# Gated linear attention and a squareplus MLP: logarithms a group ahead, second-layer PSUM banks of their own, smaller groups

## The chip, the cores and the metric

One core of a Trainium2 chip. The metric is the device time of one execution in microseconds. The engines are TensorE (PE, with its weight loads PEld), VectorE (DVE), ScalarE (ACT), GpSimd (POOL) and SyncE (SP), which here only issues DMAs.

## The reference

Attention with a decaying state, 4 batches of 8 heads, 768 steps, 48 dimensions, then an MLP with the activation squareplus:

```python
f = 1.0 / (1.0 + np.exp(-f_logit))
for t in range(S):
    state = f[:, :, t, :, None] * state + np.einsum('bhd,bhe->bhde', k[:, :, t], v[:, :, t])
    y[:, :, t] = np.einsum('bhd,bhde->bhe', q[:, :, t], state)
x = y.transpose(0, 2, 1, 3).reshape(3072, 384)
h = x @ w_in                                   # 384 x 2048
out = (0.5 * (h + np.sqrt(h * h + 4.0))) @ w_out   # 2048 x 384
```

## The kernel before

The 3072 tokens are 24 row blocks of 128 steps (6 for a batch), handled as 12 pairs. A recurrence over a block is a chunked matmul form: with the logarithms of the decays summed over the block, q is multiplied by one exponential and k by its inverse, and scores, state update and outputs are matmuls.

The stages of a pair:

- *Loads* (`load_pair`, L96): f, q, k and v, eight DMAs of 192 KB on SP, into four buffers each.
- *Logarithms* (`exp_ln`, L131): two ACT passes, Exp in place and Ln into `ls`, then on DVE the fp16 cast `hi` (L137, tile lhi) and the rest `lo` (L138, tile llo); POOL casts v to `v16` (L140).
- *Decays* (`cums`, L143): PE sums hi and lo within a block (L148, L149) into two of the four PSUM banks `hps`; ACT takes `ea` (L155) and `eap` (L156) from them, POOL multiplies q and k with these (L157, L158); PE then forms boundary sums in the same banks (L164, L165), DVE copies them to `nls` (L166).
- *Gammas* (`gammas`, L168), once for a group: a small DVE addition `gi` (L180) and two small Exp on ACT, `gam` (L183), which scale the state from block to block.
- *Attention* of a block, in steps that stand in slots (`attention`, L264): transposes T with an eviction to qkT (L205 to L208), scores SC with a mask multiplication pm on DVE (L218, L220), state KV (L229 to L235), outputs Y (L246 to L251), transposed back by YT (L258, L261). Every one of T, SC (twice), KV, Y, YT takes one of the four PSUM banks of the pool `pp_a`.
- *First layer* (`mlp1`, L288): for a pair 8 halves of 6 matmuls (L299) into the four hps banks; after each two halves ACT squares (L306) and takes the root (L307), and DVE forms the activation g (L310).
- *Second layer* (`mlp2`, L317): 32 matmuls (L328) in 8 quarters into an accumulator `o`, also from `pp_a`, a copy to `o_sb` (L332) and a store on SP (L334).

The pairs are in groups (`GROUPS`). For each group there is a *window* (`run_window`, L366): ACT loads the table with Exp and Ln (L367), does logarithms, decays and gammas of the group, and loads the table with Sqrt (L371). Between windows stands the *stretch* of first layers (`run_mlp1`, L376) of the group before; attention slots of the group just prepared are dealt out between its halves. Second-layer quarters wait in the list `fill`: two are issued at each step of a window, and before a pair's first layer as many as bring the list down to 24.

The order on ACT is that of the code (`manual_schedule`). The other engines and SP have a compile-time planner, which plays the program through with estimated durations and issues what is ready, older code first. Every queue is then fixed and runs in that order. Groups count row blocks: `(4, 6)` is pair 2. Windows are called here by the group's number, so that window 3 is that of pairs 3 and 4 before.

Of the kernel before, what the change touches and what calls it, by code (L numbers as in the profile page):

```python
# [14 lines left out]

GROUPS = [(0, 2), (2, 4), (4, 6), (6, 10), (10, 16), (16, 22), (22, 24)]
# [3 lines left out]
def kernel(  # L22
# [34 lines left out]
    pp_a = ctx.enter_context(tc.tile_pool(name="pp_a", bufs=4, space=PSUM))  # L57
# [20 lines left out]
    qt = [konst.tile([128, PR, H, 64], FP16, name=f"qt{i}") for i in range(NB)]  # L78
    kt = [konst.tile([128, PR, H, 64], FP16, name=f"kt{i}") for i in range(NB)]
    lhi = [konst.tile([128, PR, H, 64], FP16, name=f"lhi{i}") for i in range(2)]  # L80
    llo = [konst.tile([128, PR, H, 64], FP16, name=f"llo{i}") for i in range(2)]
# [43 lines left out]
    def window(g):  # L125

        r0, r1 = GROUPS[g]
        pairs = range(r0 // PR, r1 // PR)
        lss, steps = {}, []

        def exp_ln(p):  # L131
            f = loads[p]["f"]
            ls = wp.tile([128, PR, H, D], FP32, name="ls", tag="ls")
            nc.scalar.activation(out=f, in_=f, func=AF.Exp, scale=-1.0)
            nc.scalar.activation(out=ls, in_=f, func=AF.Ln, bias=1.0, scale=1.0)
            hi, lo = lhi[p % 2], llo[p % 2]
            nc.vector.tensor_copy(out=hi[:, :, :, 0:D], in_=ls)  # L137
            nc.vector.tensor_tensor(out=lo[:, :, :, 0:D], in0=ls, in1=hi[:, :, :, 0:D], op=ALU.subtract)  # L138
            v16 = bp.tile([128, PR, H, D], FP16, name="v16", tag="v16", bufs=4)
            nc.gpsimd.tensor_copy(out=v16, in_=loads[p]["v"])  # L140
            v16s[p] = v16

        def cums(p):  # L143
            hi, lo = lhi[p % 2], llo[p % 2]
            hp2 = [hps[2 * (p % 2) + r] for r in range(PR)]
            for r in range(PR):
                ca = hp2[r][:, 0:H * D]
                nc.tensor.matmul(out=ca, lhsT=wcent, rhs=hi[:, r, :, 0:D], start=True, stop=False)  # L148
                nc.tensor.matmul(out=ca, lhsT=wcent, rhs=lo[:, r, :, 0:D], start=False, stop=True)  # L149
            ea = wp.tile([128, PR, H, D], FP32, name="ea", tag="ea")  # L150
            eap = wp.tile([128, PR, H, D], FP32, name="eap", tag="eap")
            ld = loads[p]
            for r in range(PR):
                ca = hp2[r][:, 0:H * D]
                nc.scalar.activation(out=ea[:, r].rearrange("p h d -> p (h d)"), in_=ca, func=AF.Exp, scale=-1.0)  # L155
                nc.scalar.activation(out=eap[:, r].rearrange("p h d -> p (h d)"), in_=ca, func=AF.Exp, scale=1.0)  # L156
            nc.gpsimd.tensor_tensor(out=qt[p % NB][:, :, :, 0:D], in0=ld["q"], in1=ea, op=ALU.mult)  # L157
            nc.gpsimd.tensor_tensor(out=kt[p % NB][:, :, :, 0:D], in0=ld["k"], in1=eap, op=ALU.mult)  # L158
            b, c = divmod(p * PR, NC)
            for r in range(PR):  # L160
                nl = hp2[r][:, H * D:H * D + 2 * NP].rearrange("p (j s) -> p j s", s=2)
                for hp in range(NP):
                    o = nl[:, hp, :]
                    nc.tensor.matmul(out=o, lhsT=hi[:, r, 2 * hp:2 * hp + 2, :], rhs=hvec, start=True, stop=False)  # L164
                    nc.tensor.matmul(out=o, lhsT=lo[:, r, 2 * hp:2 * hp + 2, :], rhs=hvec, start=False, stop=True)  # L165
                nc.vector.tensor_copy(out=nls[b % 2][:, c + r], in_=nl)  # L166

        def gammas():  # L168

            a = r0  # L170
            while a < r1:
                b, c = divmod(a, NC)
                e = min(r1, (b + 1) * NC)
                n = e - a
                nb, gm = nls[b % 2], gam[b % 2]
                c0 = max(c - 1, 0)
                c1 = c + n - 1
                if c1 > c0:
                    gi = wp.tile([128, NC, NP], FP32, name="gi", tag="gi")
                    nc.vector.tensor_tensor(out=gi[:, c0:c1], in0=nb[:, c0:c1, :, 1],  # L180
                                            in1=nb[:, c0 + 1:c1 + 1, :, 0], op=ALU.add)
                    for s in range(2):
                        nc.scalar.activation(out=gm[64 * s:64 * s + 64, c0:c1, :, s],  # L183
                                             in_=gi[64 * s:64 * s + 64, c0:c1], func=AF.Exp, scale=-1.0)
                a = e

        ps = list(pairs)
        steps.append(lambda p=ps[0]: exp_ln(p))
        for i, p in enumerate(ps):
            if i + 1 < len(ps):  # L190
                steps.append(lambda p=ps[i + 1]: exp_ln(p))
            steps.append(lambda p=p: cums(p))
        steps.append(gammas)
        return steps

# [5 lines left out]
    def st_T(r):  # L201
        p, i = divmod(r, PR)
        tr = pp_a.tile([128, 2 * NP, C], FP16, name="tr", tag="a")
        for j in range(NP):
            nc.tensor.transpose(out=tr[:, j, :], in_=qt[p % NB][:, i, 2 * j:2 * j + 2, :], identity=ident16)  # L205
            nc.tensor.transpose(out=tr[:, NP + j, :], in_=kt[p % NB][:, i, 2 * j:2 * j + 2, :], identity=ident16)  # L206
        qkT = bp.tile([128, 2 * NP, C], FP16, name="qkT", tag="qkT")
        nc.vector.tensor_copy(out=qkT, in_=tr)  # L208
        part[r] = {"qkT": qkT}
# [243 lines left out]
```

## Time and profile before

| | us |
|---|---|
| median of 3 runs | 272.44 (270.02 to 272.85) |
| profiled execution, device time | 270.39 |
| its span, first to last instruction | 268.6 |
| PE busy | 213.1 |
| DVE busy | 182.7 |
| ACT busy | 169.3 |
| POOL busy | 57.5 |

Busy PE is not PE at its peak, since ends of matmuls are modelled and overlap. Times in rows count from the span's start. "Idle" beside an instruction is the time in which its engine waited just ahead of it, with what ended the wait.

### The profile page before, as it was taken

How to read it: one execution, taken by the hardware profiler on the slowest of the kernel's cores; microseconds unless marked ns; L12 is line 12 of the kernel's file. 1: busy time of each engine (PE TensorE's matmuls, PEld its weight loads, DVE VectorE, ACT ScalarE, POOL GpSimd, SP SyncE). 2: the span in 40 equal slices, each digit the busy share in tenths (PEclk: the TensorE clock that was granted, in tenths of full speed). 3: DMA queues.
4: the chain of work that ended last, by engine and by line, in shares of the span. 5: the costliest groups of instructions: out<-in, count | busy, mean ns of one | idle time of the engine just before them, and what ended most of it. 6: DMA issues, size and time to landing. Idle time of an engine off the chain costs nothing.

```text
span 268.6 us, 5160 instructions
## 1 busy us (share of the span) xinstructions
PE 213.1 (79%) x2024; PEld 148.9 (55%) x2024; DVE 182.7 (68%) x332; ACT 169.3 (63%) x252; POOL 57.5 (21%) x52
## 2 busy tenths in 40 slices
PE   0366939897688775986886869999886999999995
PEld 0143626664446553575664537777654777767652
DVE  1456726863583899579999666999983697645521
ACT  4355567884822956548968645988867795938200
POOL 4325001004209001494110396000005000000000
PEclk9999995999555997999999989999998899999999
DMA  8995599599995099999994000000000000010121
GB/s 144 187 220 184 161 234 302 153 245 188 177 216 93 8 214 185 187 217 195 166 199 76 31 32 29 2 0 4 2 29 29 2 29 33 29 59 32 59 79 70
DMA packets 107032, 30.22 MB, mean 113 GB/s; under 512 B 100352, under 2 KB 105472, under 8 KB 107008
## 3 DMA queue, kind: packets, MB, share of 16 engines
q1 hardware_dynamic: 107008, 29.89, 58.8%
q8 instruction: 16, 0.26, 0.4%
q14 instruction: 8, 0.07, 0.1%
HBM read 25.17 MB, written 4.72 MB: 111 GB/s over the span
## 4 chain that ended last, share of the span: by engine, by line
PE 32%; DVE 22%; ACT 16%; DMA 10%; issue 8%; SPq 6%; POOL 4%; POOLq 1%; ACTq 0%; DVEq 0%
PE o L328 16%; PE hps L299 10%; SPq L104 6%; DVE g L310 6%; ACT hsq L306 4%; DVE pm L220 3%; ACT r L307 3%; DMA ld_v<-in_v_dram 3%; DMA ld_f<-in_f_logit_dram 3%; DMA w_st<-in_moe_w_in_dram 3%; DVE qkT L208 2%; DVE llo L138 2%; POOL kt L158 2%; DVE y L251 2%; ACT L371 2%
## 5 line engine op out<-in xcount | busy, mean ns | idle before, releaser
L299 PE MATMUL hps<-xT,w_in 128*128 128x256 f16 x576 | 80.5, 285 | 10.6 <-DVE g L310 9.7
L310 DVE SCALAR_TENSOR_TENSOR g<-hps,r 128x512 f16<-128x512 f32 x96 | 61.8, 682 | 20.5 <-ACT r L307 20.5
L328 PE MATMUL o<-w_out,g 128*128 128x384 f16 x384 | 73.0, 335 | 0.2 <-DVE w_out L120 0.2
L299 PEld LDWEIGHTS <-w_in 128*128 128x128 f16 x576 | 57.0, 102 | 23.5 <-issue 13.2
L306 ACT ACTIVATE hsq<-hps 128x512 f16<-128x512 f32 x96 | 54.5, 590 | 23.4 <-PE hps L299 22.3
L307 ACT ACTIVATE r<-hsq 128x1024 f16<-128x1024 f16 x48 | 50.7, 1057 | 1.5
L328 PEld LDWEIGHTS <-g 128*128 128x128 f16 x384 | 37.6, 100 | 23.4 <-issue 3.3
L157 POOL TENSOR_TENSOR qt<-ld_q,ea 128x768 f16<-128x768 f32 x12 | 22.7, 1892 | 82.4 <-ACT ea L155 72.6
L220 DVE TENSOR_TENSOR pm<-sc,mask 128x512 f16<-128x512 f32 x48 | 30.9, 682 | 4.2 <-PE sc L218 4.2
L155 ACT ACTIVATE ea<-hps 128x384 f32<-128x384 f32 x24 | 11.9, 494 | 29.1 <-PE hps L149 29.1
L140 POOL CAST v<-ld_v 128x768 f16<-128x768 f32 x12 | 10.2, 853 | 65.6 <-DMA ld_v<-in_v_dram 60.7
L332 DVE COPY o_sb<-o 128x384 f32<-128x384 f32 x24 | 13.2, 554 | 16.0 <-PE o L328 16.0
L158 POOL TENSOR_TENSOR kt<-ld_k,eap 128x768 f16<-128x768 f32 x12 | 22.4, 1866 | 0.0
L208 DVE COPY qkT<-tr 128x1024 f16<-128x1024 f16 x24 | 16.4, 682 | 8.8 <-PE tr L206 8.8
L205 PE MATMUL tr<-ident,qt 128*128 128x128 f16 x96 | 16.7, 245 | 4.6 <-POOL qt L157 3.8
L206 PE MATMUL tr<-ident,kt 128*128 128x128 f16 x96 | 16.3, 246 | 4.7 <-POOL kt L158 4.7
L218 PE MATMUL sc<-qkT 48*128 48x128 f16 x192 | 12.1, 243 | 7.2 <-DVE qkT L208 7.1
L166 DVE COPY nls<-hps 128x8 f32<-128x8 f32 x24 | 3.8, 163 | 19.6 <-PE hps L165 18.6
L148 PE MATMUL hps<-lhi,wcent 128*128 128x384 f16 x24 | 8.2, 394 | 10.4 <-DVE wcent L66 8.7
L248 PE MATMUL y<-v,pm 128*128 128x48 f16 x192 | 14.1, 193 | 2.7 <-DVE pm L220 2.5
L183 ACT ACTIVATE gam<-gi 64x8 f32<-64x8 f32 (+2 forms) x18 | 3.8, 209 | 17.5 <-DVE gi L180 17.4
L206 PEld LDWEIGHTS <-kt 128*128 128x128 f16 x96 | 10.6, 111 | 7.5 <-POOL kt L158 5.8
(49 smaller groups left out, 256.0 us busy)
## 6 DMA issues: line engine op xcount, KB each, us to landing
ld_f<-in_f_logit_dram SPq DMA_DIRECT2D x24, 192.0 KB, 4.6
ld_q<-in_q_dram SPq DMA_DIRECT2D x24, 192.0 KB, 4.6
ld_k<-in_k_dram SPq DMA_DIRECT2D x24, 192.0 KB, 4.6
ld_v<-in_v_dram SPq DMA_DIRECT2D x24, 192.0 KB, 4.6
out_dram<-o_sb SPq DMA_DIRECT2D x24, 192.0 KB, 1.9
w_st<-in_moe_w_in_dram SPq DMA_DIRECT2D x4, 768.0 KB, 6.2
w_st<-in_moe_w_out_dram SPq DMA_DIRECT2D x4, 768.0 KB, 5.3
```

The costliest lines, as they stand in the source:

```text
L104: nc.sync.dma_start(out=got[name][:, r], in_=src[b][:, c * C:(c + 1) * C, :].rearrange("h t d -> t h d"))
L157: nc.gpsimd.tensor_tensor(out=qt[p % NB][:, :, :, 0:D], in0=ld["q"], in1=ea, op=ALU.mult)
L158: nc.gpsimd.tensor_tensor(out=kt[p % NB][:, :, :, 0:D], in0=ld["k"], in1=eap, op=ALU.mult)
L205: nc.tensor.transpose(out=tr[:, j, :], in_=qt[p % NB][:, i, 2 * j:2 * j + 2, :], identity=ident16)
L206: nc.tensor.transpose(out=tr[:, NP + j, :], in_=kt[p % NB][:, i, 2 * j:2 * j + 2, :], identity=ident16)
L208: nc.vector.tensor_copy(out=qkT, in_=tr)
L220: nc.vector.tensor_tensor(out=pm[:, s], in0=sc, in1=mask16.unsqueeze(1).broadcast_to([128, NP, C]), op=ALU.mult)
L299: nc.tensor.matmul(out=hb[:, a, :], lhsT=w_in16[:, j, jn * 128:(jn + 1) * 128], rhs=x[:, j, :], start=(j == 0), stop=(j == NJ - 1))
L306: nc.scalar.activation(out=hsq[:, a, :], in_=hps[(2 * j4 + a) % 4], func=AF.Square, scale=1.0)
L307: nc.scalar.activation(out=r16, in_=hsq, func=AF.Sqrt, scale=0.25, bias=1.0)
L310: nc.vector.scalar_tensor_tensor(out=g16[:, jn:jn + 2, :].rearrange("p a t -> p (a t)"), in0=hps[(2 * j4 + a) % 4], scalar=0.5, in1=r16[:, ...
L328: nc.tensor.matmul(out=o, lhsT=gts[p][:, jn, i * C:(i + 1) * C], rhs=w_out16[:, jn, :], start=(jn == 0), stop=(jn == NN - 1))
```

## The change

- Each group's logarithms are formed in the window ahead of its own (`logs`), behind that window's decays and in front of its `gammas`. hi and lo have four buffers each in place of two.
- `lo` and `gi` go from DVE to POOL; the cast `v16` goes from POOL to DVE and from the logarithms to the decays.
- Two banks of `pp_a` become a pool `pp_o` for the accumulators of the second layer; attention keeps two.
- Groups: the single pairs go on to pair 3, then four groups of two pairs; before, 2, 3, 3 and 1 pairs followed three single ones.
- From group 2 on, a stretch deals out only 80% (SHARE) of the attention slots; the rest goes into the next window, two at each of its steps from window 4 on.
- At the start one stay under the log table covers groups 0 and 1, the casts of w_in and the logarithms of pair 2; the Sqrt table is loaded behind them.
- f is loaded up to three groups ahead and q, k, v two, at the end of a window. qkT has three buffers. q and k are halves of one tile, and a DMA transpose is written down that no block reaches (XBAR_FROM is 24).

```diff
-GROUPS = [(0, 2), (2, 4), (4, 6), (6, 10), (10, 16), (16, 22), (22, 24)]
+GROUPS = [(0, 2), (2, 4), (4, 6), (6, 8), (8, 12), (12, 16), (16, 20), (20, 24)]
+SHARE = 0.8
-    pp_a = ctx.enter_context(tc.tile_pool(name="pp_a", bufs=4, space=PSUM))
+    pp_a = ctx.enter_context(tc.tile_pool(name="pp_a", bufs=2, space=PSUM))
+    pp_o = ctx.enter_context(tc.tile_pool(name="pp_o", bufs=2, space=PSUM))
+    def logs(p):
+        f = loads["f", p]
+        ls = wp.tile([128, PR, H, D], FP32, name="ls", tag="ls")
+        nc.scalar.activation(out=f, in_=f, func=AF.Exp, scale=-1.0)
+        nc.scalar.activation(out=ls, in_=f, func=AF.Ln, bias=1.0, scale=1.0)
+        hi, lo = lhi[p % NL], llo[p % NL]
+        nc.vector.tensor_copy(out=hi[:, :, :, 0:D], in_=ls)
+        nc.gpsimd.tensor_tensor(out=lo[:, :, :, 0:D], in0=ls, in1=hi[:, :, :, 0:D], op=ALU.subtract)
+    def decays(p):
...
+        nc.gpsimd.tensor_tensor(out=qt[p % NB][:, :, :, 0:D], in0=loads["q", p], in1=ea, op=ALU.mult)
+        nc.gpsimd.tensor_tensor(out=kt[p % NB][:, :, :, 0:D], in0=loads["k", p], in1=eap, op=ALU.mult)
+        v16 = bp.tile([128, PR, H, D], FP16, name="v16", tag="v16", bufs=4)
+        nc.vector.tensor_copy(out=v16, in_=loads["v", p])
...
+    def gammas(g):
...
+                nc.gpsimd.tensor_tensor(out=gi[:, c0:c1], in0=nb[:, c0:c1, :, 1],
+                                        in1=nb[:, c0 + 1:c1 + 1, :, 0], op=ALU.add)
...
-                    box["o"] = pp_a.tile([128, DM], FP32, name="o", tag="a")
+                    box["o"] = pp_o.tile([128, DM], FP32, name="o", tag="o")
...
+    def window(g, g_logs, per=2, slots=1):
+        nc.scalar.preload_act_table_set("natural_log_exp_and_others")
+        for p in pairs_of[g]:
+            decays(p)
+            for _ in range(slots):
+                att_slot()
             fill_some(per)
+        for h in g_logs:
+            for p in pairs_of[h]:
+                logs(p)
+                for _ in range(slots):
+                    att_slot()
+                fill_some(per)
+        gammas(g)
         nc.scalar.preload_act_table_set("sqrt_and_others")
         att.extend(attention(g))
+        loads_upto(pairs_of[min(g + 3, NG - 1)][-1] + 1, pairs_of[min(g + 2, NG - 1)][-1] + 1)
...
+    logs(0)
+    decays(0)
+    gammas(0)
+    logs(1)
+    decays(1)
+    gammas(1)
+    att += attention(0)
+    att += attention(1)
+    for i in range(2):
         load_w_in(i)
+    loads_upto(3, 2)
+    logs(2)
+    for i in range(2, 4):
+        load_w_in(i)
+    loads_upto(3, 3)
+    nc.scalar.preload_act_table_set("sqrt_and_others")
     while att:
         att_slot()
+    run_mlp1(0, 1)
     for i in range(4):
         load_w_out(i)
+    loads_upto(5, 5)
+    run_mlp1(1, 1)
+    window(2, [3], 2, 0)
     while att:
         att_slot()
         fill_some(2)
+    window(3, [4], 2, 0)
+    run_mlp1(2, SHARE)
     for g in range(3, NG):
         if g + 1 < NG:
+            window(g + 1, [g + 2] if g + 2 < NG else [], 2, 2)
+        run_mlp1(g, SHARE if g + 1 < NG else 1)
```

## Rows read from the trace of the kernel before

**Rows 1.** Page, busy us (share of the span) and instructions of each engine

```profile
PE 213.1 (79%) x2024; PEld 148.9 (55%) x2024; DVE 182.7 (68%) x332; ACT 169.3 (63%) x252; POOL 57.5 (21%) x52
```

**Rows 2.** Busy time by stage, cut at ACT's table loads and first squares

```profile
core 0: us, PE busy (x) PEld busy (x) DVE busy (x) ACT busy (x) POOL busy (x), PEclk, DMA share, GB/s
...
68.30:89.00 20.70, 16.77 (x146) 11.12 (x147) 12.64 (x23) 9.56 (x17) 8.69 (x6) 0.55 0.87 147
89.00:100.65 11.65, 8.46 (x116) 6.62 (x115) 11.20 (x23) 8.56 (x12) 0.00 (x0) 1.00 0.63 127
100.65:123.40 22.75, 17.43 (x192) 11.80 (x194) 18.56 (x33) 13.04 (x25) 13.36 (x9) 0.92 1.22 196
123.40:144.50 21.10, 17.05 (x219) 13.18 (x219) 20.51 (x39) 17.23 (x25) 2.35 (x3) 1.00 1.19 179
144.50:166.25 21.75, 17.41 (x160) 10.83 (x162) 15.46 (x26) 12.98 (x24) 12.41 (x7) 0.92 0.08 28
166.25:196.00 29.75, 27.41 (x336) 21.90 (x332) 29.23 (x55) 26.45 (x37) 0.14 (x1) 1.00 0.01 2
196.00:206.05 10.05, 6.66 (x61) 4.05 (x58) 5.90 (x12) 6.30 (x11) 3.57 (x2) 1.00 0.11 39
206.05:250.80 44.75, 43.74 (x359) 32.05 (x360) 28.43 (x48) 33.64 (x48) 0.00 (x0) 0.96 0.08 28
250.80:268.60 17.80, 14.51 (x90) 8.51 (x87) 4.64 (x8) 0.00 (x0) 0.00 (x0) 0.98 0.22 78
```

**Rows 3.** Timeline of ACT, windows 2 and 3: start us, us, instruction [idle before]

```profile
58.33 1.28 ACT L367 ACT_TABLE_LOAD   x1
...
68.33 1.28 ACT L367 ACT_TABLE_LOAD   x1
69.62 0.84 ACT L134 ACTIVATE ld_f<-ld_f 128x768 f32<-128x768 f32 x1
...
72.11 0.84 ACT L135 ACTIVATE ls<-ld_f 128x768 f32<-128x768 f32 x1
78.77 0.49 ACT L155 ACTIVATE ea<-hps 128x384 f32<-128x384 f32 x1 [5.82 <-PE hps L149]
...
79.89 0.51 ACT L156 ACTIVATE eap<-hps 128x384 f32<-128x384 f32 x1
...
87.26 0.44 ACT L183 ACTIVATE gam<-gi 64x12 f32<-64x12 f32 x2 [5.12 <-DVE gi L180]
```

**Rows 4.** Waits, engine and line <- releaser: us in total, times, longest

```profile
ACT ea L155 <- PE hps L149: 29.1, 11, 5.8
...
ACT gam L183 <- DVE gi L180: 17.4, 7, 5.1
```

**Rows 5.** Groups of instructions: busy us, mean ns | idle before, releaser

```profile
L310 DVE SCALAR_TENSOR_TENSOR g<-hps,r 128x512 f16<-128x512 f32 x96 | 61.8, 682 | 20.5 <-ACT r L307 20.5
L328 PE MATMUL o<-w_out,g 128*128 128x384 f16 x384 | 73.0, 335 | 0.2 <-DVE w_out L120 0.2
...
L306 ACT ACTIVATE hsq<-hps 128x512 f16<-128x512 f32 x96 | 54.5, 590 | 23.4 <-PE hps L299 22.3
L307 ACT ACTIVATE r<-hsq 128x1024 f16<-128x1024 f16 x48 | 50.7, 1057 | 1.5
...
L157 POOL TENSOR_TENSOR qt<-ld_q,ea 128x768 f16<-128x768 f32 x12 | 22.7, 1892 | 82.4 <-ACT ea L155 72.6
...
L138 DVE TENSOR_TENSOR llo<-ls,lhi 128x768 f16<-128x768 f32 x12 | 12.9, 1090 | 0.2
...
L140 POOL CAST v<-ld_v 128x768 f16<-128x768 f32 x12 | 10.2, 853 | 65.6 <-DMA ld_v<-in_v_dram 60.7 <-PE hps L299 3.8 <-PE u L232 1.1
```

**Rows 6.** By tile (lhi) and line (gi): ns min/median/max

```profile
L137 DVE CAST lhi<-ls x12: 547/556/2060, 6.8 to 199.0; 128x768 f16<-128x768 f32 x12
L138 DVE TENSOR_TENSOR llo<-ls,lhi x12: 945/954/2441, 7.4 to 199.6; 128x768 f16<-128x768 f32 x12
...
L180 DVE TENSOR_TENSOR gi<-nls x9: 643/809/1750, 11.9 to 203.6; 128x8 f32<-128x8 f32 x5, 128x12 f32<-128x12 f32 x3, 128x4 f32<-128x4 f32 x1
```

**Rows 7.** SP's issue of pair 5's f, and time to landing of all f

```profile
69.43 1.84 SPq L104 DMA_DIRECT2D ld_f<-in_f_logit_dram  x2
...
DMA to landing us min/median/max: 3.1/4.6/8.0
```

**Rows 8.** Timeline of POOL in the window from 144.5

```profile
152.36 1.82 POOL L157 TENSOR_TENSOR qt<-ld_q,ea 128x768 f16<-128x768 f32 x1 [14.82 <-ACT ea L155]
...
158.00 2.51 POOL L158 TENSOR_TENSOR kt<-ld_k,eap 128x768 f16<-128x768 f32 x1
```

More of the change, by code (lines that the diff above doesn't have):

```diff
@@ L13 @@
 PSUM = bass.MemoryType.PSUM
-GROUPS = [(0, 2), (2, 4), (4, 6), (6, 10), (10, 16), (16, 22), (22, 24)]
+XBAR_FROM = 24
+GROUPS = [(0, 2), (2, 4), (4, 6), (6, 8), (8, 12), (12, 16), (16, 20), (20, 24)]
+SHARE = 0.8
 @with_exitstack
@@ L77 @@
     NB = 4
[L78 to L81, printed above, removed]
+    NL = 4
+    qk = [konst.tile([128, PR, 2, H, 64], FP16, name=f"qk{i}") for i in range(NB)]
+    qt = [t[:, :, 0] for t in qk]
+    kt = [t[:, :, 1] for t in qk]
+    lhi = [konst.tile([128, PR, H, 64], FP16, name=f"lhi{i}") for i in range(NL)]
+    llo = [konst.tile([128, PR, H, 64], FP16, name=f"llo{i}") for i in range(NL)]
     gam = [konst.tile([128, NC, NP, 2], FP32, name=f"gam{i}") for i in range(2)]
@@ L123 @@
     v16s = {}
-    def window(g):
-        r0, r1 = GROUPS[g]
[L128 to L194, printed above, removed]
@@ new lines, in gammas @@
+    def gammas(g):
+        r0, r1 = GROUPS[g]
+        a = r0
+        while a < r1:
+            b, c = divmod(a, NC)
+            e = min(r1, (b + 1) * NC)
+            n = e - a
+            nb, gm = nls[b % 2], gam[b % 2]
+            c0 = max(c - 1, 0)
+            c1 = c + n - 1
+            if c1 > c0:
+                gi = wp.tile([128, NC, NP], FP32, name="gi", tag="gi")
+                nc.gpsimd.tensor_tensor(out=gi[:, c0:c1], in0=nb[:, c0:c1, :, 1],
+                                        in1=nb[:, c0 + 1:c1 + 1, :, 0], op=ALU.add)
+                for s in range(2):
+                    nc.scalar.activation(out=gm[64 * s:64 * s + 64, c0:c1, :, s],
+                                         in_=gi[64 * s:64 * s + 64, c0:c1], func=AF.Exp, scale=-1.0)
+            a = e
@@ L202, in st_T @@
         p, i = divmod(r, PR)
[L203 to L208, printed above, removed]
+        qkT = bp.tile([128, 2 * NP, C], FP16, name="qkT", tag="qkT", bufs=3)
+        if r < XBAR_FROM:
+            tr = pp_a.tile([128, 2 * NP, C], FP16, name="tr", tag="a")
+            for j in range(NP):
+                nc.tensor.transpose(out=tr[:, j, :], in_=qt[p % NB][:, i, 2 * j:2 * j + 2, :], identity=ident16)
+                nc.tensor.transpose(out=tr[:, NP + j, :], in_=kt[p % NB][:, i, 2 * j:2 * j + 2, :], identity=ident16)
+            nc.vector.tensor_copy(out=qkT, in_=tr)
+        else:
+            nc.sync.dma_start_transpose(out=qkT, in_=qk[p % NB][:, i].rearrange("p a h d -> p (a h d)"))
         part[r] = {"qkT": qkT}
@@ L255, in st_YT @@
         p, i = divmod(r, PR)
-        yt = pp_a.tile([128, NJ, C], FP16, name="yt", tag="a")
-        for j in range(NJ):
-            nc.tensor.transpose(out=yt[:, j, :], in_=part[r]["y16"][:, j, :], identity=ident16)
         if i == 0:
             xTs[p] = xp.tile([128, NJ, TB], FP16, name="xT", tag="xT")
-        nc.vector.tensor_copy(out=xTs[p][:, :, i * C:(i + 1) * C], in_=yt)
+        xo = xTs[p][:, :, i * C:(i + 1) * C]
+        if r < XBAR_FROM:
+            yt = pp_a.tile([128, NJ, C], FP16, name="yt", tag="a")
+            for j in range(NJ):
+                nc.tensor.transpose(out=yt[:, j, :], in_=part[r]["y16"][:, j, :], identity=ident16)
+            nc.vector.tensor_copy(out=xo, in_=yt)
+        else:
+            nc.sync.dma_start_transpose(out=xo, in_=part[r]["y16"].rearrange("p a b -> p (a b)"))
         del part[r]
```

76 lines of the change are left out of this document (42 added, 34 removed).

## The prediction

> **What bounds the kernel now.** The page's busy shares come first [rows 1]: PE 79%, DVE 68%, ACT 63%. No engine is full, so the time is lost where one stage waits for another. ACT is the engine to cut the span by, because its order is the code's own: every group goes through a window (log/exp table, between two table loads) and then a stretch of first-layer elements (sqrt table). The busy time by stage, cut at those points, shows which is which [rows 2]. The windows of 22.75 us (pairs 5 to 7) and 21.75 us (pairs 8 to 10) hold only 13.0 us of ACT work each. The stretch from 166.25 is full on DVE (29.23 of 29.75 us), that from 206.05 on PE (43.74 of 44.75), and the end from 250.8 is PE's second layer alone. So a window is a chain of waits, a stretch is work. The stage 68.3 to 89.0 is the worst: 9.56 us of ACT in 20.7, and a granted clock of 0.55, near the lower level (1.2 GHz).
>
> The list of waits names the two gaps of a window [rows 4]: ACT waits 29.1 us for the centred sums (ea behind matmul L149) and 17.4 us for the boundary sums (gam behind gi on DVE, 2.5 us each in 7 waits). ACT's timeline shows both in window 3 [rows 3]: logarithms from 69.62 to 72.95 (72.11 + 0.84), then 5.82 us of nothing until the first ea at 78.77, ea and eap until about 82.1, then 5.12 us of nothing until gam at 87.26.
>
> **The change, part by part.** The sum is made against the profiled run: 268.6 us of span, 270.39 us of device time, so 1.8 us lie around it. That run is 2.05 us below the median of 272.44.
>
> *Logarithms one group ahead.* The casts to hi and lo and the sums behind them leave the window in which they are used: at its head the matmuls L148/L149 need only old data and free hps banks. What goes is the first gap, 29.1 us over 11 waits. It can't all come back: what is late next is gi. Each window still pays two table loads of 1.28 us [rows 3]; by the code there are 14 before and 14 after, since the first two windows merge and a later one is added.
>
> *gi and llo go to POOL, v16 to DVE.* On DVE 12.9 us of llo (12 by 1.09 [rows 5]; median 0.954 [rows 6]) and 9 gi of 0.64 to 1.75 us [rows 6] go, and 12 casts come. A cast of v16's size is lhi's: 0.556 us median [rows 6], so 6.7 us; off the chain, since windows leave DVE room [rows 2]. On POOL 12 casts of 0.853 [rows 5] go and 12 subtractions come. POOL has no such row for fp16 and fp32 inputs; its multiply of the same 128x768 takes 1.89 us [rows 5], and I take 1.88.
>
> That makes POOL the chain of a window with two pairs of decays and two of logarithms, counted from its first table load:
> - ACT: 1.28 + 3.36 for two pairs of ea/eap (78.77 to 79.89 and 0.51 is 1.63; two pairs about 3.36) + 3.33 for two pairs of logarithms (69.62 to 72.95) = 8.0 us, then gam.
> - POOL: the first qt starts when both ea are there, 1.3 us behind the first one, so at 2.6; four multiplies of 1.88 end at 10.1. The v16 casts hold it up as other casts did in the window from 144.5, where two multiplies took 1.82 and 2.51 us [rows 8]; with 0.56 for each of two, 11.2. gi is tiny; between POOL's and DVE's rows I take DVE's shortest, 0.64 [rows 6]: 11.8.
> - If the planner keeps the order of the code, both llo (and two hi casts' holds) stand ahead of gi: + 3.8 + 1.1, 16.7.
>
> So ACT waits 3.8 to 8.7 us for gi. The row that it is nearest to is the longest gi wait before, 5.12 us [rows 3], in a window with two pairs; I take 5.1, so gi at 13.1, gam 0.44, sqrt load 1.28: **14.8 us**. The last window has no logarithms: 11.8 + 1.7 = 13.5. Behind the waiting gam on ACT stands the whole next stretch; PE and DVE can meanwhile do the 20% of attention steps that SHARE leaves over, and the first four hps banks.
>
> *Windows 4 to 7.* Before, three windows cost 22.75 + 21.75 + 10.05 = 54.55 us [rows 2]. After: 3 x 14.8 + 13.5 = 57.9. **+3.3 us.** This part gains nothing by itself: fewer waits in each, but one window more.
>
> *Up to window 3.* The sqrt load now stands behind the last w_in cast in front of the first square: +1.3 us. Its cover, the wait for weights, is gone there. Window 2 starts at 59.6 in place of 58.33 [rows 3] and lasts about 10 us as before (POOL: 2.6 + 2 x 1.88 + 0.56 + gi, with or without one llo; bounds 9.2 and 11.7). Window 3 opens at 69.7: table load 71.0, decays of pair 3 to 72.6 (its loads were issued by 60 us), logarithms of pair 4 to 74.3. Those of pair 5 wait for f5: SP issues it at 69.43 to 71.27 in the same order behind the same weights, and it lands 4.6 us later (3.1 to 8.0) [rows 7], at 75.9. ACT waits for it with gam, the sqrt load and the stretch behind. Then 1.7 of logarithms, 0.44, 1.28, and half of one more POOL operation: 79.9 against 89.0. **-9.1 us** (f5 from 74.4 to 79.3: -10.6 to -5.7). This is the gain: pair 4 no longer sits in the window that pair 2's stretch waits for.
>
> *SHARE, smaller groups, stretches.* The stretches took 11.65 + 21.1 + 29.75 + 44.75 = 107.25 us for ten pairs and 18 blocks of attention [rows 2]. In the full one a block cost DVE (29.23 - 24 x 0.68)/6 = 2.15 us (24 squareplus outputs g of 0.68 [rows 5], six blocks). After, in 1, 1, 2, 2 and 4 pairs, with 20% of the blocks in windows: 10, 10.8, 19, 19, a little under the old lengths per pair (11.65, and 29.75/3 = 9.9). The last four pairs are PE's and hold four blocks where there were two; PE was the less busy engine in the full stretch, so a block costs it under 2.15, 1.4 taken: 44.75 + 2.8 = 47.5. Sum 106.3, **-0.9 us** (bounds: -6, if 20% of 14 blocks at 2.15 all counts, and +4, if none does and PE pays 2.15 and more).
>
> *Banks, buffers, loads.* The second layer has waited 0.2 us in 384 matmuls [rows 5], so its own banks give nothing. For what attention's loss of two costs, nothing is the lower bound (a rival has the upper). NL, three qkT buffers and the reordered loads cost nothing: f slots come free at Ln, a window earlier than the rest, so later loads are asked for a whole group ahead, under stretches of 19 us and more; without that cover a window would wait as window 3 does. The transpose by DMA is never reached, as XBAR_FROM is 24. The tail keeps 24 quarters (96 matmuls): 0.
>
> Sum: -9.1 + 3.3 - 0.9 = -6.7; 268.6 becomes 261.9 of span, 263.7 us of device time. Against the median it may read up to 2 us more: **264 us**.
>
> **The rivals.**
> *gi comes early.* Planner and POOL put gi between the multiplies, and nothing waits: a window is 8.0 + 0.44 + 1.28 = 9.7, the last 6.4, 35.5 in all, -19 in place of +3.3. DVE takes some back: it has (182.7 - 12.9 - 9.0 + 6.7)/12 = 14 us for a pair, so at 90% two pairs take 31 us, and window and stretch (9.7 + 19) can't be 28.7: +6.9 for three. -9.1 - 19 + 6.9 - 0.9 = -22.1, 248 us by the profiled run, **250 us** against the median. For it: the planner issues what is ready first, and gi is tiny. Against: POOL has a multiply ready at every moment up to 10.1.
>
> *The change does not shorten windows at all.* gi last at 16.7: 18.4 a window, 68.7 in all, +14.1. The stretches behind find DVE's backlog done and shrink to ACT's time, 17.5 us for 19 (eight squares and four roots of 54.5/96 and 50.7/48 us for a pair [rows 5]), -4.5 in three: 14.1 - 4.5 - 9.1 - 0.9 = -0.4, 270 to **272 us**. For it: order of the code, and stretched POOL rows (2.51 for 1.82 [rows 8]) and a cast of 2.060 for 0.556 [rows 6]. Beside these rows stands a rule of the Trainium skill, SBUF — State Buffer, section Who interferes with whom: a VectorE cast in a two-port mode and a GpSimd instruction exclude each other for the whole of one instruction. The trace agrees with it (2.060 against 0.556). By that rule all four casts of a window, not two, hold POOL up, 1.1 us more in each of three windows: the sum would be 267 and not 264.
>
> *Two banks throttle attention (slower).* A block needs six banks in turn. With two, a bank comes back after its eviction and what DVE has ahead of it; with one g of 0.68 [rows 5] ahead, 6/2 x 1.36 = 4.1 us a block, where a stretch of 19 us has 3.2 blocks, 5.9 for each. From two g's ahead (6.1) it decides; at 2.5 g's it is 7.1, +1.2 us by 14.4 blocks in stretches, 17 us: **281 us**. For it: DVE is full in the stretch from 166.25 [rows 2], and PE's queue is in order, so that first-layer matmuls stand behind a waiting transpose. Against: ACT feeds a pair's eight g in 8.8 us, one each 1.1.
>
> **How the numbers follow.** Forecast 0.48 (alone 256 to 270: f5, the gi bounds and the stretches); gi early 0.18; no shorter windows 0.18; two banks 0.16. The measurement tells about 1% from no change, 2.7 us. Faster by over 1%: 0.48 + 0.18 = 0.66; within: 0.18; slower: 0.16. The range leaves out the slow case and the edges of the others: 250 to 274.
>
> **What would show it.** The first square behind window 3 near 80 us (wrong: after 84). gam waiting for POOL gi, 4 to 9 us, in the later windows, and ea hardly waiting for L149 (under 10 us in all, from 29.1). llo near 1.9 us on POOL. PE idle behind pm and qkT evictions in stretches, longer than before, would speak for the banks. If f5 is issued earlier than 69, or behind an output store, the largest term is wrong; if gi runs between the multiplies, the second.

## The result and the profile after

The changed kernel takes 258.26 us (median of 4 runs, 255.81 to 259.67), the kernel before, timed beside it, 271.25: a ratio of 0.9488, 95% interval 0.9385 to 0.9591. The forecast was 264 (250 to 274). The profiled execution took 255.81 us of device time, its span is 253.7 us. It is the fastest of the four, so the terms below add up to more (14.9 us) than the medians differ by (13.0). Ratios and their intervals leave out runs of a slower state, so they are not always the quotients of the medians.

The page's busy time per engine, to be read beside [rows 1]:

```profile
PE 209.2 (82%) x2024; PEld 149.6 (59%) x2024; DVE 177.4 (70%) x327; ACT 168.7 (66%) x252; POOL 71.8 (28%) x61
```

The engines have hardly less to do: PE 3.9 us less, DVE 5.3, ACT 0.6, and POOL 14.3 more. The span is 14.9 us shorter because stages wait less. The busy time by stage, cut at the same points as [rows 2] (start:end and length in us, busy us of PE, PEld, DVE, ACT and POOL, then the granted clock):

```profile
68.59:77.94 9.35, 7.59 (x95) 5.72 (x94) 8.43 (x15) 7.99 (x13) 5.71 (x4) 0.84 0.38 90
77.94:92.57 14.63, 12.27 (x111) 8.82 (x110) 11.14 (x21) 8.56 (x12) 1.64 (x1) 0.87 1.10 184
92.57:105.01 12.44, 9.53 (x103) 6.46 (x102) 6.50 (x14) 9.31 (x16) 9.81 (x7) 1.00 1.14 185
105.01:115.72 10.71, 10.51 (x110) 7.88 (x108) 9.66 (x18) 8.68 (x12) 1.41 (x1) 0.84 1.21 206
115.72:128.41 12.69, 11.63 (x152) 8.42 (x150) 11.07 (x23) 9.43 (x17) 10.06 (x6) 1.00 0.96 168
128.41:147.19 18.78, 16.76 (x181) 12.87 (x176) 16.63 (x30) 16.86 (x24) 1.73 (x2) 1.00 0.85 137
147.19:160.05 12.86, 10.35 (x133) 7.24 (x132) 11.81 (x22) 9.71 (x18) 10.18 (x8) 1.00 0.08 30
160.05:179.72 19.67, 19.67 (x197) 14.70 (x197) 17.41 (x31) 17.29 (x24) 1.74 (x1) 0.91 0.01 3
179.72:191.74 12.02, 8.69 (x109) 6.01 (x108) 8.09 (x18) 6.17 (x12) 7.61 (x5) 0.97 0.10 34
191.74:236.00 44.26, 44.14 (x400) 32.77 (x399) 32.56 (x58) 34.03 (x48) 0.00 (x0) 0.97 0.07 24
236.00:253.70 17.70, 14.39 (x89) 8.44 (x87) 4.54 (x8) 0.00 (x0) 0.00 (x0) 0.96 0.22 79
```

Windows and stretches alternate, beginning with window 3 in the first row. Set against [rows 2], us:

| term | before | after | change | forecast |
|---|---|---|---|---|
| up to the first square behind window 3 | 89.0 | 77.94 | -11.1 | -9.1 |
| windows 4 to 7 (three before) | 54.55 | 50.01 | -4.5 | +3.3 |
| stretches | 107.25 | 108.05 | +0.8 | -0.9 |
| end | 17.8 | 17.7 | -0.1 | 0 |
| sum | | | -14.9 | -6.7 |

The list of waits (us in total, times, longest), the answer to [rows 4]:

```profile
ACT gam L182 <- POOL gi L179: 24.0, 8, 5.8
ACT ea L151 <- PE hps L146: 8.6, 6, 3.6
```

The wait for the centred sums fell from 29.1 us to 8.6, the one for the boundary sums rose from 17.4 to 24.0. ACT's timeline through window 3 and the stretch behind it, the answer to [rows 3]:

```profile
68.59 1.28 ACT L369 ACT_TABLE_LOAD   x1
70.30 0.49 ACT L151 ACTIVATE ea<-hps 128x384 f32<-128x384 f32 x1 [0.43 <-PE hps L146]
...
74.01 0.83 ACT L133 ACTIVATE ld_f<-ld_f 128x768 f32<-128x768 f32 x1
...
76.15 0.42 ACT L182 ACTIVATE gam<-gi 64x4 f32<-64x4 f32 x2 [0.38 <-POOL gi L179]
76.59 1.28 ACT L382 ACT_TABLE_LOAD   x1
77.94 0.60 ACT L303 ACTIVATE hsq<-hps 128x512 f16<-128x512 f32 x1
...
79.49 1.06 ACT L304 ACTIVATE r<-hsq 128x1024 f16<-128x1024 f16 x1
...
87.60 0.60 ACT L303 ACTIVATE hsq<-hps 128x512 f16<-128x512 f32 x1 [4.99 <-PE hps L296]
```

Window 3 has hardly a gap left; a new one of 4.99 us stands in the stretch behind it, where ACT waits for a first layer.

### The profile page after: what moved, and what is told of

It reads as the page before. It is cut to its first block, busy times and chain, and to the rows that moved or that the text cites. A ratio compares the mean times of both kernels' runs of the same rounds, so it can differ in the third digit from the quotient of the medians.

```text
span 253.7 us, 5203 instructions
## 1 busy us (share of the span) xinstructions
PE 209.2 (82%) x2024; PEld 149.6 (59%) x2024; DVE 177.4 (70%) x327; ACT 168.7 (66%) x252; POOL 71.8 (28%) x61
## 4 chain that ended last, share of the span: by engine, by line
PE 33%; issue 22%; POOL 14%; ACT 10%; DVE 7%; DMA 6%; SPq 4%; POOLq 1%; ACTq 0%; DVEq 0%
PE hps L296 14%; PE o L325 13%; POOL qk L154 5%; POOL qk L153 4%; SPq L109 4%; DVE g L307 3%; ACT r L304 3%; DMA w_st<-in_moe_w_in_dram 3%; POOL llo L137 3%; ACT hsq L303 2%; PE sc L211 2%; DMA ld_f<-in_f_logit_dram 2%; DMA ld_q<-in_q_dram 2%; POOL gi L179 1%; DVE pm L213 1%
## 5 line engine op out<-in xcount | busy, mean ns | idle before, releaser
L325 PE MATMUL o<-w_out,g 128*128 128x384 f16 x384 | 79.9, 330 | 0.0
L153 POOL TENSOR_TENSOR qk<-ld_q,ea 128x768 f16<-128x768 f32 x12 | 22.2, 1854 | 93.8 <-ACT ea L151 51.0
L137 POOL TENSOR_TENSOR llo<-ls,lhi 128x768 f16<-128x768 f32 x12 | 20.1, 1688 | 23.8 <-DVE lhi L136 23.7
L211 PE MATMUL sc<-qkT 48*128 48x128 f16 x192 | 18.8, 232 | 9.4 <-DVE sn L228 5.9
L154 POOL TENSOR_TENSOR qk<-ld_k,eap 128x768 f16<-128x768 f32 x12 | 23.6, 1965 | 0.0
L329 DVE COPY o_sb<-o 128x384 f32<-128x384 f32 x24 | 13.1, 551 | 12.6 <-PE o L325 12.6
L211 PEld LDWEIGHTS <-qkT 48*128 48x128 f16 x192 | 10.8, 99 | 18.4 <-issue 10.9
L182 ACT ACTIVATE gam<-gi 64x4 f32<-64x4 f32 (+3 forms) x18 | 3.8, 208 | 24.1 <-POOL gi L179 24.0
L198 PE MATMUL tr<-ident,qk 128*128 128x128 f16 x96 | 16.3, 248 | 4.0 <-POOL qk L154 4.0
L197 PE MATMUL tr<-ident,qk 128*128 128x128 f16 x96 | 16.8, 247 | 2.3 <-POOL qk L153 2.0
L228 DVE TENSOR_TENSOR sn<-u,gam 128x384 f16<-128x384 f32 x20 | 11.0, 552 | 6.7 <-ACT gam L182 5.2
L136 DVE CAST lhi<-ls 128x768 f16<-128x768 f32 x12 | 11.9, 1006 | 4.7 <-ACT ls L134 4.7
```

What stands on the lines that cost most here:

```text
L137: nc.gpsimd.tensor_tensor(out=lo[:, :, :, 0:D], in0=ls, in1=hi[:, :, :, 0:D], op=ALU.subtract)
L153: nc.gpsimd.tensor_tensor(out=qt[p % NB][:, :, :, 0:D], in0=loads["q", p], in1=ea, op=ALU.mult)
L154: nc.gpsimd.tensor_tensor(out=kt[p % NB][:, :, :, 0:D], in0=loads["k", p], in1=eap, op=ALU.mult)
L211: nc.tensor.matmul(out=sc[:, j, :], lhsT=qkT[o:o + D, NP + j, :], rhs=qkT[o:o + D, j, :], start=True, stop=True)
```

## Experiments

All times are medians of four runs. "Before" ran beside each, at 271.25 to 272.94 us.

| kernel | us | ratio to before (95%) |
|---|---|---|
| the change | 258.26 | 0.9488 (0.9385 to 0.9591) |
| before, new groups only | 263.28 | 0.966 (0.9593 to 0.9726) |
| the change, old engines, banks and SHARE | 260.15 | 0.9582 (0.9539 to 0.9625) |
| the change, old groups | 279.55 | 1.0293 (1.0224 to 1.0362) |
| the change, logarithms in their own window | 280.55 | 1.0315 (1.0225 to 1.0406) |
| the change, lo on DVE | 259.44 | 0.9554 (0.9493 to 0.9615) |
| the change, gi on DVE | 257.8 | 0.9378 (0.9276 to 0.948) |
| the change, SHARE 1 | 260.54 | 0.9599 (0.955 to 0.9647) |
| the change, four shared banks | 264.72 | none, see below |
| the change, four shared banks and SHARE 1 | 266.45 | 0.9732 (0.9644 to 0.9819) |
| the change, banks 3 and 1 | 259.68 | 0.9505 (0.9439 to 0.9571) |
| banks 3 and 1, gi on DVE | 254.81 | 0.9334 (0.9265 to 0.9403) |
| the same, last outputs in attention's banks | 250.41 | 0.9207 (0.9124 to 0.9291) |

### Which part carries it: groups, logarithms, or both

The kernel before with nothing but the new groups:

```diff
-GROUPS = [(0, 2), (2, 4), (4, 6), (6, 10), (10, 16), (16, 22), (22, 24)]
+GROUPS = [(0, 2), (2, 4), (4, 6), (6, 8), (8, 12), (12, 16), (16, 20), (20, 24)]
```

> The kernel before with nothing changed but its group list, which becomes the new one. If the largest term (window 3 no longer holds pair 4) needs only the groups: the first square behind window 3 falls from 89 to about 80 us, but each of the later four windows keeps both gaps at two table loads, so 262 to 267 us. If the groups need the logarithms ahead to pay: 270 to 276, as one window more eats what window 3 gives.

263.28 us: the groups alone, with each group's logarithms still at the head of its own window, give 8.6 us of the 13. Window 3 holds one pair there instead of two, and its first square stands at 83.95, not at the 80 expected.

The changed kernel with lo and gi back on DVE, v16 on POOL, SHARE 1 and four shared banks, so that the logarithms ahead (with the merged first windows and the new loads) stand alone on top of the groups:

```diff
-SHARE = 0.8
+SHARE = 1
-        nc.gpsimd.tensor_tensor(out=lo[:, :, :, 0:D], in0=ls, in1=hi[:, :, :, 0:D], op=ALU.subtract)
+        nc.vector.tensor_tensor(out=lo[:, :, :, 0:D], in0=ls, in1=hi[:, :, :, 0:D], op=ALU.subtract)
...
```

> The new groups with the logarithms a group ahead, but lo and gi on DVE, the cast of v on POOL, four shared banks and SHARE at 1, all as before. Beside it stand 263.3 us for the kernel before with the new groups alone and 258.3 for the full change. If logarithms ahead by themselves make the rest of the gain: 256 to 260. If they need the banks (shared ones cost 264.7 in the changed kernel) or the engines: 262 to 267.

260.15 us, no run of it (259.67 to 260.83) as long as any of the groups alone (262.84 to 263.75). So the logarithms ahead are worth some 3 us there. Engines, banks and SHARE together give about 2 more by the medians, but the intervals overlap. With gi and lo on DVE and no attention left over, windows 4 to 7 take only 42.1 us (9.32, 12.03, 10.93 and 9.86) against 50.0 in the change, but the three stretches between them take 60.2 instead of 49.2.

The changed kernel with the old groups:

> The changed kernel with the old group list: pairs 3 and 4 together, then 3, 3 and 1. If the largest term is right (pair 2's stretch must not wait for the data of later pairs): window 3 holds two pairs of decays and three of logarithms, the last of them needs pair 7's f, and its first square comes at 88 to 95 us in place of 78: 268 to 278 us. If logarithms ahead make the group sizes irrelevant: 256 to 261.

279.55 us, slower than before and above what was expected; the first square behind window 3 comes at 103.14, expected at 88 to 95. ACT's timeline in that window:

```profile
91.18 0.84 ACT L133 ACTIVATE ld_f<-ld_f 128x768 f32<-128x768 f32 x1 [14.85 <-DMA ld_f<-in_f_logit_dram]
...
99.72 0.84 ACT L133 ACTIVATE ld_f<-ld_f 128x768 f32<-128x768 f32 x1 [6.77 <-DMA ld_f<-in_f_logit_dram]
```

Formed a group ahead, the logarithms of three pairs sit in the window of two, and wait for f of pairs whose loads have not come: 21.6 us of ACT. That is the wait that the forecast set for f5, on a larger scale. SP's timeline shows why the first of them comes so late; its second line is the issue of pair 6's f:

```profile
79.17 0.36 SPq L331 DMA_DIRECT2D out_dram<-o_sb  x1
...
85.45 2.02 SPq L109 DMA_DIRECT2D ld_f<-in_f_logit_dram  x2
```

The issue stands in SP's queue behind an output store and q, k and v of pair 5. So with these loads the logarithms can stand ahead only of small groups; whether large ones would do with every f asked for earlier was not tried.

The changed kernel with the logarithms at the head of their own window, all else kept:

```diff
     def window(g, g_logs, per=2, slots=1):
...
         for p in pairs_of[g]:
+            logs(p)
+            for _ in range(slots):
+                att_slot()
+            fill_some(per)
+        for p in pairs_of[g]:
             decays(p)
...
-        for h in g_logs:
...
-    logs(2)
```

> The changed kernel with each group's logarithms at the head of its own window instead of a window ahead (pair 2's too); groups, banks, engines and SHARE as changed. If logarithms ahead are what shortens the windows: each of windows 4 to 7 gets back the gap ahead of the first ea, an ls, a cast and a subtraction on POOL of 1.64 us per pair, 3 to 5 us, and window 2 the 3 us that hid behind the weights: 272 to 280 us. If the smaller groups alone make the gain: 256 to 262.

280.55 us. ACT's timeline in its window 3, which opens at 71.61:

```profile
73.78 0.84 ACT L134 ACTIVATE ls<-ld_f 128x768 f32<-128x768 f32 x1
81.71 0.49 ACT L151 ACTIVATE ea<-hps 128x384 f32<-128x384 f32 x1 [7.09 <-PE hps L146]
...
86.80 0.42 ACT L182 ACTIVATE gam<-gi 64x4 f32<-64x4 f32 x2 [3.46 <-POOL gi L179]
```

Both waits stand in the window one behind the other: in the whole run 24.1 us for the centred sums and 35.4 for gi. POOL's lo (1.66 us, against DVE's 1.09 [rows 5]) is now on the chain of the window, and the multiplies follow it. The kernel with the groups alone waits 27.2 and 14.1 us at the same two places, so what grew is the wait for gi, which stands in POOL's queue here. The engines of the change therefore seem to depend on the logarithms ahead; banks and SHARE differ between these two kernels as well, and were not taken back one by one.

### The engines of lo and gi

lo back on DVE:

> The changed kernel with the subtraction lo back on DVE, all else as changed. If taking it off DVE relieves the engine that fills the stretches: 12 subtractions of 0.95 us return, 261 to 265 us. If it is off the path, as the windows leave DVE room and POOL does llo behind gi and the stretches run on without it: 256 to 260. POOL's chain up to gi stays as it is, so windows 4 to 7 should stay near 12.5 us by both.

259.44 us, within the change's own runs; gam still waits for gi 24.4 us (24.0 with lo on POOL). lo on POOL stood behind gi and held up nothing that shows in the time.

gi back on DVE:

```diff
-                nc.gpsimd.tensor_tensor(out=gi[:, c0:c1], in0=nb[:, c0:c1, :, 1],
+                nc.vector.tensor_tensor(out=gi[:, c0:c1], in0=nb[:, c0:c1, :, 1],
```

> The changed kernel with gi on DVE again, all else as changed. gam waits 24.0 us for gi on POOL, where gi stands behind the last multiply. If that wait sets the windows' length: gi runs behind nls on DVE, in 0.6 to 1.8 us beside POOL's multiplies, under the logarithms; windows 4 to 6 shorten by 2.5 each, window 7 by 3 to 5: 246 to 252 us. If PE and DVE give it back in the stretches: 256 to 260. If gi on DVE stands behind attention's evictions or POOL's port: over 261.

257.8 us, and the intervals overlap: no difference shown. Its waits:

```profile
ACT gam L182 <- DVE gi L179: 17.8, 6, 4.5
ACT ea L151 <- PE hps L146: 14.2, 5, 5.4
```

gam waits 6.2 us less, since gi need not stand behind POOL's multiplies, but ea waits 5.6 us more. Windows 4 to 7 take 46.7 us instead of 50.0, as the first expectation had it, but window 3 takes 15.12 instead of 9.35, and the stretches are longer too. (This profile is of a run with a granted clock of 0.934, that of the change has 0.950.)

### SHARE and the banks

SHARE of 1, so that a stretch deals out all its attention:

> The changed kernel with SHARE at 1: stretches deal out all attention slots, none is left for the windows. If the 20% in the windows is a gain (forecast: up to 6 us of DVE time): 260 to 264 us, with longer stretches and windows of the same 12.5 us. If it only moves work that is hidden in both: 256 to 260.

260.54 us, some 2 us longer than the change by the medians, and its runs (259.75 to 261.74) lie just above the change's, while the intervals overlap. The fifth left to the windows is worth that or nothing.

Outputs back in four banks shared with attention:

```diff
-    pp_a = ctx.enter_context(tc.tile_pool(name="pp_a", bufs=2, space=PSUM))
-    pp_o = ctx.enter_context(tc.tile_pool(name="pp_o", bufs=2, space=PSUM))
+    pp_a = ctx.enter_context(tc.tile_pool(name="pp_a", bufs=4, space=PSUM))
```

> The changed kernel with the second layer's accumulators back in the attention pool, four banks for both, as before the change. If the forecast's term (the banks give nothing and cost nothing) holds: 256 to 261 us, as the changed kernel's 258. If two banks throttle attention: ACT's wait of 4.99 us in the stretch of pair 2 goes and the stretches shorten, 251 to 255. If an accumulator that sits in one of four shared banks is what the own pool cures: 262 to 268, with PE waiting for evictions in windows.

264.72 us, in runs far apart: one took 258.92 with a granted clock of 0.967, the other three 263.66 to 265.79 with 0.922 to 0.935, and the profile is of one of these three. The same with SHARE 1, to see whether leftover attention in the windows competes for the banks:

> The changed kernel with second-layer outputs back in the four shared banks (as e1) and SHARE back at 1 (as e6). Theory A, the shared banks cost because attention matmuls that SHARE of 2 leaves between the first layers compete with the second layer's outputs for the same banks: with SHARE 1 that competition goes and the time is that of the SHARE edit alone, 259 to 261 us. Theory B, shared banks cost by themselves: 263 to 267 us.

266.45 us, so theory A fell: SHARE is not what makes shared banks cost. The busy time of the kernel with shared banks (SHARE 0.8), from its window 2 to its first ea in window 3 (at 74.72), shows where it is lost:

```profile
62.00:64.00 2.00, 0.75 (x12) 0.42 (x10) 1.40 (x3) 1.80 (x3) 2.00 (x2) 1.00 1.31 185
64.00:66.77 2.77, 1.85 (x16) 1.15 (x14) 2.23 (x2) 0.42 (x2) 2.75 (x3) 0.55 1.39 191
66.77:74.50 7.73, 7.73 (x38) 3.95 (x36) 3.47 (x6) 2.57 (x2) 1.18 (x1) 0.50 0.79 161
```

The granted clock falls soon after 64.00 to 0.50, the lower level of 1.2 GHz, and stays there until 74.50. In the 2.00 us up to 64.00 PE was busy for 0.75. In the change it was busy for 1.54 of these, and the clock is 1.00 from 59.82 to 68.59:

```profile
62.00:64.00 2.00, 1.54 (x22) 0.88 (x21) 0.83 (x3) 1.97 (x4) 1.55 (x1) 1.00 1.32 187
```

At the lower level PE works through attention and second-layer matmuls that stand ahead of pair 3's centred sums, and the first ea waits 5.37 us. With shared banks, SHARE 1 and the old engines (260.15 us above) the whole is 6 us shorter again. The queues of a kernel are fixed, and yet one run of four took 258.92 us, as the change does, at a higher clock. So what shared banks cost comes with a lower clock; that they cost where the clock stays up isn't shown, and why it falls in some runs and in some orders of work stays open.

Three banks for attention and one for outputs:

```diff
-    pp_a = ctx.enter_context(tc.tile_pool(name="pp_a", bufs=2, space=PSUM))
-    pp_o = ctx.enter_context(tc.tile_pool(name="pp_o", bufs=2, space=PSUM))
+    pp_a = ctx.enter_context(tc.tile_pool(name="pp_a", bufs=3, space=PSUM))
+    pp_o = ctx.enter_context(tc.tile_pool(name="pp_o", bufs=1, space=PSUM))
```

> The changed kernel with three banks for attention and one for the second layer's outputs, in place of two and two. Theory A, two attention banks throttle the stretch behind window 3 (14.63 us, with 4.99 us of ScalarE waiting for a first layer): that wait falls to under 2 us and the time to 253 to 256 us. Theory B, a single output bank stalls the second layer for each copy out: TensorE waits there, 260 to 264 us. Theory C, the wait is VectorE's order and neither counts: 256 to 260 us with the 4.99 us still there.

259.68 us, as the change, but out of two effects. The stage from the last window's end to the end of the run, to be read beside the last two rows of the change, which add up to 61.96 us:

```profile
188.98:258.40 69.42, 59.78 (x494) 41.25 (x493) 37.36 (x66) 34.12 (x48) 0.00 (x0) 1.00 0.11 38
```

Up to there three banks are 2.8 us ahead (188.98 against 191.74, one profile of each); then one output bank costs 7.5. The time is in the range of theory C, but the 4.99 us are not still there; of A and B each holds in part. The long wait in pair 2's stretch shrinks from 4.99 to 3.04 us, but ACT's waits for first layers in that stretch only from 5.9 to 5.6: a bank was not its main cause.

The same with gi on DVE:

> As e10, and the products for the state's decay back on VectorE (as e4). If the bank split and the engine of these products act apart from each other, the time is that of e10 less 0 to 1 us; if the order on VectorE behind window 3 is what counts, 1 to 3 us more than e10.

254.81 us, 4.9 less: more than either expectation. The last window ends at 182.36 instead of 188.98, and the four windows take 46.6 us instead of 49.7. With two attention banks the same edit shortened the windows by as much and showed nothing in the time; why it pays with three isn't shown. PE's timeline at its end:

```profile
228.53 2.76 PE L325 MATMUL o<-w_out,g 128*128 128x384 f16 x16 [0.65 <-DVE o_sb L329]
231.94 2.76 PE L325 MATMUL o<-w_out,g 128*128 128x384 f16 x16 [0.65 <-DVE o_sb L329]
```

Each output block takes 3.41 us, with 0.65 of PE waiting for the copy out of the only bank. No attention is left by then, so its banks are free. Outputs begun from there on are put into them:

```diff
-                    box["o"] = pp_o.tile([128, DM], FP32, name="o", tag="o")
+                    late = len(done_x) == NRB
+                    box["o"] = (pp_a if late else pp_o).tile([128, DM], FP32, name="o", tag="a" if late else "o")
```

> As the kernel with three attention banks, one output bank and the decay products on VectorE, but outputs begun when no attention is left go to the three attention banks. Theory A, the single bank's price is the tail's: an output block takes 3.41 us there, of which 0.65 is TensorE waiting for the copy out, against 2.60 with two banks. Then six to eight blocks gain about 0.8 us each, 5 us in all, and the time is 248 to 251 us. Theory B, with banks in turn the copies or the stores bound the tail: 253 to 256 us. A sum that shows this would be the stretch from the last table load to the end: 69.2 us before this edit, 63 to 65 by theory A.

250.41 us (249.4 to 250.94), theory A; its interval stands clear of the change's. The last stage takes 63.94 us instead of 69.24 (5.3 of the 7.5 us come back), and PE's timeline closes without a gap:

```profile
229.23 16.41 PE L326 MATMUL o<-w_out,g 128*128 128x384 f16 x100
```

This is the fastest version: the change with three banks for attention while there is attention, one for outputs until then and three after it, and gi on DVE.

## Why the prediction was right in sign and short in size

**Up to window 3: right, and a little short.** The largest term was to come from pair 4 leaving the window that pair 2's stretch waits for. The first square stands at 77.94 us, forecast near 80. The run of the groups alone has it at 83.95, that with the logarithms ahead but the old engines, banks and SHARE at 78.95: so the groups give 5 of the 11 us, the logarithms ahead 5 and the rest 1. The clock has a part in this that was not taken out: window 3 ran at 0.55 before [rows 2], at 0.60 with the groups alone (below), at 0.73 in the run with 78.95 and at 0.84 in the change. What failed is the step that f5 would arrive at 75.9 and be waited for. SP's issue of it, timeline of SP:

```profile
66.57 2.64 SPq L331 DMA_DIRECT2D out_dram<-o_sb  x2
69.27 1.19 SPq L109 DMA_DIRECT2D ld_f<-in_f_logit_dram  x2
```

It left when forecast (69.43 [rows 7]), in 1.19 us instead of 1.84, and pair 5's first logarithm runs at 74.01 without a wait, just ahead of the lower bound of 74.4. It also stands behind an output store, which by the prediction's own sign should have undone the term; it did not, as the store was done at 69.21. What ended the window instead is gi on POOL, 0.38 us behind ACT's own logarithms. The wait itself is real: where the window opens earlier, it is there. Timeline of ACT in the fastest version, whose window 3 opens at 62.94:

```profile
72.36 0.84 ACT L133 ACTIVATE ld_f<-ld_f 128x768 f32<-128x768 f32 x1 [2.13 <-DMA ld_f<-in_f_logit_dram]
```

The prediction's term ended at the first square, and that was where it stopped looking. Window 3 and the stretch behind it with the groups alone:

```profile
68.59:83.95 15.36, 11.60 (x106) 8.15 (x106) 8.04 (x16) 6.30 (x11) 4.42 (x4) 0.60 1.14 197
83.95:93.60 9.65, 7.40 (x87) 5.35 (x87) 8.53 (x15) 8.56 (x13) 0.74 (x1) 1.00 0.18 42
```

From the opening of window 3 to that of window 4 the change takes 23.98 us (68.59 to 92.57) and the groups alone 25.01 (68.59 to 93.60): 5 of the 6 us gained in the window are given back in the stretch behind it.

**Windows 4 to 7: the step that failed.** The forecast was 57.9 us, the measurement 50.0. The mis-sized term is gi's time, taken as 13.1 us behind the table load, between 11.8 and 16.7. Timeline of POOL in window 4, which opens at 92.57:

```profile
95.20 1.82 POOL L153 TENSOR_TENSOR qk<-ld_q,ea 128x768 f16<-128x768 f32 x1 [10.43 <-ACT ea L151]
96.98 1.81 POOL L154 TENSOR_TENSOR qk<-ld_k,eap 128x768 f16<-128x768 f32 x1
98.76 2.20 POOL L153 TENSOR_TENSOR qk<-ld_q,ea 128x768 f16<-128x768 f32 x1
100.92 2.12 POOL L154 TENSOR_TENSOR qk<-ld_k,eap 128x768 f16<-128x768 f32 x1
103.00 0.22 POOL L179 TENSOR_TENSOR gi<-nls 128x16 f32<-128x16 f32 x1
103.18 3.23 POOL L137 TENSOR_TENSOR llo<-ls,lhi 128x768 f16<-128x768 f32 x2
```

The chain is the one forecast: the first multiply starts at 2.63 us (2.6 forecast), four multiplies in a row, then gi. But gi ends at 10.65, under the lower bound; in windows 5 to 7 it ends at 10.91, 11.09 and 10.24. The four multiplies with what the casts held them up took 7.8 us (95.20 to 103.00), where 8.6 were allowed; gi took 0.22 us, where 0.64 was read off DVE; and both llo stand behind it. The 5.12 us wait of [rows 3] was the wrong row to lean on: it came from a chain on DVE that the change takes apart. gam waited 2.89, 2.60 and 2.54 us in windows 4 to 6, under the 4 to 9 forecast, and 5.80 in the last, inside it. With the groups alone these four windows take 57.5 us (13.69, 17.49, 14.49 and 11.87), what the forecast gave the whole change: the 7.5 us are what the rest of the change takes out of them.

**Stretches: near in sum, by two errors.** 108.05 us measured, 106.3 forecast. Pair 2's stretch was set at 10 and took 14.63. Timeline of DVE in it, where ACT has the first root ready at 80.55 (79.49 + 1.06):

```profile
81.83 0.69 DVE L199 COPY qkT<-tr 128x1024 f16<-128x1024 f16 x1 [0.70 <-PE tr L198]
82.44 0.55 DVE L136 CAST lhi<-ls 128x768 f16<-128x768 f32 x1
...
83.92 1.29 DVE L213 TENSOR_TENSOR pm<-sc,mask 128x512 f16<-128x512 f32 x2
85.13 0.35 DVE L256 COPY xT<-yt 128x384 f16<-128x384 f16 x1
85.39 1.28 DVE L307 SCALAR_TENSOR_TENSOR g<-hps,r 128x512 f16<-128x512 f32 x2
```

The g of that root starts at 85.39, 4.8 us later, behind attention's evictions and a cast of pair 5; until it has read its two hps banks the next first layer can't be written into them, and ACT gets its next square at 87.60. The forecast priced DVE's work of a stretch but not its order. That the evictions stand there because window 3, 11 us shorter, had no room for them is the reading that fits; it was not tried by itself. The last stretch was set at 47.5 and took 44.26: four blocks of attention beside four pairs of PE's work cost no more than two had before (44.75 [rows 2]), where 1.4 us a block was taken.

**Banks.** "Its own banks give nothing" was argued from a wait of 0.2 us [rows 5]. That row says only that PE did not stand waiting for a bank at that line, in that order of its queue; the 0.2 us themselves are a wait for w_out. With shared banks the changed kernel is 6 us longer by the medians, in runs at a lower granted clock. Attention's loss of two banks had nothing as its lower bound and 17 us as the rival's price. One bank more is worth 2.8 us up to the last stage, by one profile of each; four for attention beside a pool for outputs were not tried. PE's own waits behind qkT's evictions, which would have spoken for the rival, fell from 7.1 us to 3.9.

**The rivals.** gi did come ahead of llo, but behind the multiplies (in window 6, whose group spans two batches, the first of two gi stands between them and the second behind), so the windows lie between the forecast's and that rival's 35.5. The rival with no shorter windows and the slower one did not come about. The other forecasts that could be read off held: ea waits 8.6 us (under 10), and llo takes 1.69 us on average (near 1.9).

## What to carry to other kernels

Sum a chain from the producer's queue, in the order in which it will run (here multiplies, gi, llo), and not from the length of a wait in the old chain. A stage that loses its waits hands its neighbours work that had been done in them: cost the stage and the one behind it together. A split of banks may be right for one phase only: here a single output bank is enough while attention runs, and costs 5 us when only outputs are left.

## What the runs showed of the hardware

Casts on DVE were longer beside POOL's work than the forecast allowed. By tile (ns min/median/max), the cast hi of the change:

```profile
L136 DVE CAST lhi<-ls x12: 549/664/2159, 6.8 to 156.1; 128x768 f16<-128x768 f32 x12
```

Its mean is 1.006 us, and that of v16, which came to DVE, 0.894: 12 v16 casts cost DVE 10.7 us and not the 6.7 forecast from [rows 6]. One cast hi stands ahead of the late g in pair 2's stretch. A multiply on POOL took 1.82 us in window 4 ahead of these casts and 2.20 beside them. The Trainium skill, SBUF — State Buffer, section Who interferes with whom, says that a two-port cast on VectorE and a GpSimd instruction exclude each other for a whole instruction; the cast's maximum of 2.159 us is its shortest, 0.549, and 1.61 more, about one operation of POOL (1.64 to 1.82), which agrees.

The same gi is short on POOL and not on DVE. Its rows, first of the change, then of the kernel with gi on DVE:

```profile
L179 POOL TENSOR_TENSOR gi<-nls x9: 198/514/537, 15.3 to 189.7; 128x4 f32<-128x4 f32 x3, 128x8 f32<-128x8 f32 x3, 128x16 f32<-128x16 f32 x2, 128x12 f32<-128x12 f32 x1
```

```profile
L179 DVE TENSOR_TENSOR gi<-nls x9: 148/1054/1612, 12.8 to 192.7; 128x4 f32<-128x4 f32 x3, 128x8 f32<-128x8 f32 x3, 128x16 f32<-128x16 f32 x2, 128x12 f32<-128x12 f32 x1
```

On DVE an addition of at most 16 elements a partition takes 0.15 us at best and 1.6 at worst, about as long as one operation of POOL. That section of the skill also says that a DVE instruction with two inputs in SBUF contends with a GpSimd instruction that reads there, and these rows agree. Even so DVE was the better place for gi with three attention banks (254.81 against 259.68 us); on POOL it stands behind all four multiplies.
